# One sparse-attention and two-MoE kernel: a new hand-written order for the attention half, and the first loads put into one queue

## The chip, the cores and the metric

One Trainium2 chip, one core. The metric is the time of one execution of the whole program in microseconds (us); 0.2% of it is 2.2 us.

## The reference

```python
def _attn_ref(q, k, v, tau):              # q, k, v: (4, 8, 576, 64) float32
    scores = (1 / np.sqrt(64)) * np.matmul(q, k.transpose(0, 1, 3, 2))
    thresh = np.max(scores, axis=-1, keepdims=True) - tau
    scores = np.where(scores >= thresh, scores, -1000000000.0)
    scores = scores - np.max(scores, axis=-1, keepdims=True)
    attn = np.exp(scores)
    attn = attn / (np.sum(attn, axis=-1, keepdims=True) + 1e-09)
    return np.matmul(attn, v)

def _moe_ref(x, w_gate, w_val, w_out):    # x: (2304, 512), d_ff 1536
    return (1 / (1 + np.exp(-(x @ w_gate)))) * (x @ w_val) @ w_out

def _moe2_ref(x, w_in, w_out):            # d_ff 2048
    h = x @ w_in
    return (h * np.cos(h)) @ w_out

def reference(...):                       # attention -> (tokens, 512) -> moe -> moe2
    x = attn_out.transpose(0, 2, 1, 3).reshape(B * S, H * D)
    return _moe2_ref(_moe_ref(x, ...), ...)
```

The weights of the two MoE layers come in as float64.

## The kernel before

The 32 heads are worked in 16 **pairs** of heads. A pair has nine blocks of 128 queries: four for each head and one that holds the last 64 queries of both. Every product is made with split numbers: a float is a high part that TensorE takes in one pass and a low part, and two or three products are summed in PSUM.

The steps of one query block, with the letter that the tables of the kernel give them:

- S, four matmuls of 288 columns (six for the ninth block) into two PSUM banks, of which there are two pairs (L959, TensorE);
- M, the row's largest score (L965, VectorE, 128x576); E, the exponential (L970, ScalarE); Y, the threshold from M and tau (L813 on ScalarE, L817 on VectorE or L815 on GpSimd, by the table YS); K, mask, product and sum in one instruction (L973, VectorE);
- T and t, four transposes and one (L989, L996, TensorE); H and h, their high part copied out of PSUM (L899, ScalarE);
- the low part, by the table LOWS (LOWS_L for the small ones): V is a subtraction on VectorE (letters L and l, L910), G a copy on ScalarE (C, L914) and a subtraction on GpSimd (G, L919), T a matmul with minus the identity (N and n, L903, TensorE) and a copy on ScalarE (O and o, L906).

V is the product with the values (L1056, TensorE), folded by F on ScalarE and A on VectorE (L1026, L1031). R, U, X and x (L1136, L1147, L1163 to L1169) scale a pair's result and split it for the MoE product. Ahead of each pair its queries, keys and values are loaded, scaled (s), split into high (Q, J, Z) and low (q, j, z) parts and, but for the first pair, copied by DMA into the doubled layout that S reads (u, y, d). WHERE says for each pair which engine takes such a step (A ScalarE, D VectorE, P GpSimd). The letters 4, 5 (VectorE), w, 6 (ScalarE) and 7 (GpSimd) turn float64 weights into split floats. P are the matmuls of the first MoE layer (L564 to L566) that are laid between the pairs once two chunks of x are there, e their copies (L1214). D are four transposes into a spare bank that nothing reads (L825), put in after a block's S by the table FILL.

The class Plan collects these steps as tasks with what each needs. ORDER is a hand-written table: one string of letters for each engine, and the instructions of the attention half are issued on each engine in just that order. An engine works in order: an instruction that waits holds up all behind it. The second half (the rest of the MoE layers) has a table of its own, LATER.

The first pair has no DMA copies. `Pair.begin` issues its loads: tau (0.5 KB) and the first 128 queries (64 KB) on SyncE's queue, the first 640 key columns (320 KB) on ScalarE's queue; the other three pieces follow as tasks on SyncE's queue. VectorE makes `factor_q` and `off` from tau (L739, L740), ScalarE makes the high parts (`first_hi`: keys L657, queries L655, which read `factor_q`), VectorE the low parts (`first_lo`: L670, L674), GpSimd the plain key copy (`first_keys`, L683). Before that, TensorE makes 26 transposes of the identity into a bank that nothing reads:

```python
    for _ in range(26):
        nc.tensor.transpose(warm[:, 0:P], ident, ident)
```

Of the kernel before, what the change touches and what calls it, by code (L numbers as in the profile page):

```python
# [33 lines left out]
KW = 2 * S + SL  # L34
# [37 lines left out]
    DVE=(
        "jqMjqKqMMKKM4MK5MKYKMlMYYK4LL5MKYKllMMYlK4K5IlMMLKKM4l5KMMLKKlMML4K5KllMLMKLAYIlM4K5KMAMKLxlMA4KK5MYlMKxLM4K"
        "llK5MMYlLKKAM4lAI5KMLMYKK4M5MlKKLLMMAlKKALLLM4llM5IlKKLMA4l5MKAYKLMlMLKKLlMMKKALLAMllMKlAYKMLYAKIMLMlYKKLMMK"
        "lLKMMYlKKMALLllKAMMlLKKAMIlAMYKKlLMMLYKKMlAMKLYKAMLLlYlKMMlKYLKIlMMAKKAMLMlKKMMYKLAlMYLKKllLLMlAMLKKIMALMlAK"
        "KLMlMLKKLMlMYKKMMAllLLAKALKMLAMYlIKLKMMKYKMlYLKMLAYlMAKLLLMKllLKMMlLYKKIlAMMYLKKMjYlMAKKLMMlYKAKMLMKLLYAKllM"
        "YlMLLKIKlLAMMYYKKlMMALqKAlKMLLLAKMllMKLlMKAILKAlMMYYKKMlMYKYAKlAMLMKKMlYMlKKLMlMLKKIlAMMYKYKLMMAlKLMYlYKKMzA"
        "lKlMLLMAlYYILKKLlAMMYLYKKMMAlKYAKLMAlYKMLYLMllKKlMMKKLMMAlLIKKLMYlKAlMYMKYKALLAMMllAKKlILxlLAAUxAUxx"
    ),
    POOL=(  # L80
        "JJQYJYjYqZYzG7csQq7YJjYY7GYZ7YYzcGsQJ7qjUYsGXz7YQcUX7YqYJG7Y7jYYsYcQGZYqz7YJGY7GY7GjYUXZxYYsczQUXxGqJZYzYGjs"
        "cQGYJGYYqYGGYGjYsUcXYGQxZzJqGUXGxYjZYGQGqczYYZjsUXxYGzYcGGYYZUXxqzGYJjcGqYYGYJGcZzYqUGZzJjGYsGQGYZcUzXXxYxYJ"
        "GjGGGcYUYGsJjQGqYUYXxxGYGcsYQJqGzjGGGUcZGYGzUYGYGGGcYYGURRX"
    ),
    SP=(
        "10001W2uuuyWyuyy0ddssssW1uduuuW2ssssdyyrrW0y1RyssssRW2uu0uussssWrr1ddRRWyyy2yssssuuWgguu0Wssdssyydgg1WgyygDs"
        "sssrrWyggu2RRuugdrssrssuyd0RRyssssyggDu1u2d0gusygsrugss1dryyygsssysgRg2uuRu0dssssdg1ygurrgsgyyssRRsDuugg0ddu"
        "s2sssr1urygyyyDgg0ssssu2uRRyugyugDysssrrysgdg2ssssRRdu1gug0ssdrssdgguu2yDDgsyyrysssg10uuddRgssRssuugygyyy12s"
        "usssdguDrdryug0Ryussssr2rggD1RyssssdyRguu2uyRssss1yyudy0gsgDgssrrgRRs1gdys0gsdyrgrssguuuuDssyyDssgg2dgRRssss"
        "gg2uugrrdyyyuyusssRgsgRDssDssssssgrrRRgggDD"  # L90
# [1904 lines left out]
```

## Time and profile before

| | us |
|---|---|
| median of 3 runs | 1091.14 |
| lowest, highest | 1090.83, 1092.13 |
| the profiled execution, its own time | 1091.87 |
| its span | 1090.0 |
| TensorE busy | 1069.9 (98%) |
| VectorE busy | 911.8 (84%) |
| ScalarE busy | 763.3 (70%) |
| GpSimd busy | 545.0 (50%) |

The span is cut by what is done: attention and the first product up to about 385 us, the rest behind. PE, DVE, ACT, POOL and SP are TensorE, VectorE, ScalarE, GpSimd and SyncE; PEld are TensorE's weight loads. A busy share is an average, so each stretch is read by itself; in a row of the timeline the brackets tell how long the engine had been idle before an instruction, and what ended that. The 1.87 us between the span and the execution's time lie outside the profile.

### The profile page before, as it was taken

The page shows a single profiled execution, that of the slowest core. Times are in us where ns is not written, and L with a number is a line of the kernel's source. Part 1 is how long each engine was busy: PE and PEld are TensorE (multiplying, and loading weights), DVE is VectorE, ACT ScalarE, POOL GpSimd, SP SyncE. Part 2 cuts the span into 40 slices and gives each one's busy share as a digit, 9 for nine tenths or more (in the row PEclk, how much of TensorE's full clock was granted, in tenths as well). Part 3 has the DMA queues.
Part 4 walks back from the last instruction along what each step waited for, and adds up shares of the span by engine and source line. Part 5 has one row for each costly group of instructions (what it writes and reads, how often), then busy time and mean ns, then how long its engine had stood idle before and what let it go on. Part 6 is the DMA issues. An engine that isn't in the chain of part 4 may idle for free.

```text
span 1090.0 us, 17697 instructions
## 1 busy us (share of the span) xinstructions
PE 1069.9 (98%) x5774; PEld 911.6 (84%) x5774; DVE 911.8 (84%) x1650; ACT 763.3 (70%) x1488; POOL 545.0 (50%) x518
## 2 busy tenths in 40 slices
PE   7899999999999999999999999999999999999998
PEld 6788888888888888988888888888888888888886
DVE  7999998999888747878887657788779899889997
ACT  6999888888888744656654334368867677788773
POOL 6877877736775425342424252242344535445562
PEclk9999999999999999999999999999999999999999
DMA  6888788787777378998977554866444454557752
GB/s 194 233 227 243 223 225 229 203 234 219 209 203 201 94 231 305 302 335 305 312 232 232 178 180 149 282 210 215 157 155 155 159 185 159 195 192 276 265 203 87
DMA packets 94413, 234.05 MB, mean 215 GB/s; under 512 B 13178, under 2 KB 21490, under 8 KB 84594
## 3 DMA queue, kind: packets, MB, share of 16 engines
q1 hardware_dynamic: 94178, 232.60, 67.0%
q8 instruction: 46, 0.75, 0.3%
q14 instruction: 45, 0.37, 0.1%
q10 hardware_dynamic: 144, 0.33, 0.1%
HBM read 141.33 MB, written 59.84 MB: 185 GB/s over the span
## 4 chain that ended last, share of the span: by engine, by line
PE 85%; DVE 6%; ACT 3%; POOL 2%; DMA 2%; issue 2%; SPq 0%; ACTq 0%; DVEq 0%; POOLq 0%
PE h L1441 7%; PE h L1442 7%; PE h L1443 7%; PE s L959 6%; PE o L564 5%; PE o L565 5%; PE o L566 5%; PE v L1056 5%; PE h L1630 4%; PE t L989 4%; PE h L1631 4%; PE h L1632 4%; PE o L1750 4%; PE o L1751 4%; PE o L1752 4%; PE m L564 2%
## 5 line engine op out<-in xcount | busy, mean ns | idle before, releaser
L1676 POOL TENSOR_TENSOR g<-raws,g 128x512 fp32r<-128x512 f32 x68 | 94.6, 1400 | 139.8 <-ACT g L1675 117.7
L965 DVE TENSOR_REDUCE sm<-s 128x1 f32<-128x576 f32 x144 | 106.6, 751 | 9.5 <-PE s L959 7.5
L973 DVE SCALAR_TENSOR_TENSOR p<-s,sm,p 128x576 f32<-128x576 f32 x128 | 102.8, 813 | 8.8 <-ACT p L970 3.9
L1441 PE MATMUL h<-x,w 128*128 128x256 f32 (+1 forms) x304 | 101.4, 333 | 0.4 <-DVE raws L1718 0.4
L1442 PE MATMUL h<-x,w 128*128 128x256 f32 (+1 forms) x304 | 101.3, 333 | 0.0
L1443 PE MATMUL h<-x,w 128*128 128x256 f32 (+1 forms) x304 | 101.3, 333 | 0.0
L970 ACT ACTIVATE p<-s,sm 128x576 f32<-128x576 f32 x128 | 93.7, 741 | 9.8 <-DVE sm L965 9.2
L899 ACT ACTIVATE PT<-t 128x512 fp32r<-128x512 f32 (+1 forms) x160 | 86.1, 556 | 15.0 <-PE t L989 10.4
L959 PE MATMUL s<-kk,qh 128*128 128x288 f32 x320 | 92.3, 319 | 3.1 <-DVE p L973 2.0
L1056 PE MATMUL v<-PT,vn 128*128 128x256 f32 (+3 forms) x532 | 84.8, 302 | 0.2 <-ACT st L1214 0.2
L919 POOL TENSOR_TENSOR PT<-praw,PT 128x512 fp32r<-128x512 f32 x51 | 67.1, 1317 | 34.3 <-ACT praw L914 16.3
L1760 DVE TENSOR_TENSOR y<-o,y 128x512 f32<-128x512 f32 x120 | 78.7, 682 | 6.1 <-PE o L1752 5.9
L959 PE MATMUL s<-khi,ql 128*128 128x288 f32 x288 | 81.2, 296 | 1.0 <-DVE ql L670 0.6
L989 PE MATMUL t<-ident,p 128*128 128x128 f32 x512 | 76.9, 276 | 3.1 <-DVE PT L910 1.6
L1750 PE MATMUL o<-g,w 128*128 128x512 f32 x196 | 76.7, 392 | 0.5 <-ACT o L1766 0.5
L1751 PE MATMUL o<-g,w 128*128 128x512 f32 x196 | 76.4, 390 | 0.0
L1752 PE MATMUL o<-g,w 128*128 128x512 f32 x196 | 76.3, 389 | 0.0
L1630 PE MATMUL h<-form,w 128*128 128x512 f32 x192 | 75.0, 390 | 0.5 <-ACT side L1599 0.5
L1056 PEld LDWEIGHTS v<-PT,vn 128*128 128x128 f32 (+1 forms) x532 | 73.3, 186 | 2.2 <-DVE x L1031 0.5
L1631 PE MATMUL h<-form,w 128*128 128x512 f32 x192 | 74.7, 389 | 0.0
L1632 PE MATMUL h<-form,w 128*128 128x512 f32 x192 | 74.7, 389 | 0.0
L1675 ACT ACTIVATE g<-raws 128x512 fp32r<-128x512 f32 x106 | 64.3, 624 | 13.1 <-DVE raws L1718 8.3
(214 smaller groups left out, 3385.5 us busy)
## 6 DMA issues: line engine op xcount, KB each, us to landing
w<-wd SPq DMA_DIRECT2D x62, 1024.0 KB
wd<-stage SPq DMA_DIRECT2D x64, 512.0 KB
gd<-st SPq DMA_DIRECT2D x64, 256.0 KB
wraw<-in_moe_w_out_dram SPq DMA_DIRECT2D x28, 512.0 KB
qh<-qsplit SPq DMA_DIRECT2D x60, 144.0 KB
wraw<-in_moe_w_in_dram SPq DMA_DIRECT2D x16, 512.0 KB
spare<-gd SPq DMA_DIRECT2D x7, 1024.0 KB
early<-gd SPq DMA_DIRECT2D x7, 1024.0 KB
```

What stands on the lines that cost most here:

```text
L959: nc.tensor.matmul(s[:, half, 0:HALF], qq, keys[:, half * HALF:half * HALF + HALF], start=(i == 0), stop=(i == len(mms) - 1),)
L989: nc.tensor.matmul(tp[:, c * P:(c + 1) * P], self.pn[:, k0:k0 + P], ident, is_transpose=True, start=(c == 0), stop=(c == 3))
L1056: nc.tensor.matmul(o, w, x, start=z == 0, stop=z == len(steps) - 1)
L1441: nc.tensor.matmul(o, w_hi, x(0, c), start=begin, stop=False, **late)
L1442: nc.tensor.matmul(o, w_hi, x(1, c), start=False, stop=False, **late)
L1443: nc.tensor.matmul(o, w_lo, x(0, c), start=False, stop=c == KC - 1, **late)
L1630: nc.tensor.matmul(ps(), of(0, c), hi, start=fresh and c == 0, stop=False, skip_group_check=True)
L1631: nc.tensor.matmul(ps(), of(0, c), lo, start=False, stop=False, skip_group_check=True)
L1632: nc.tensor.matmul(ps(), of(1, c), hi, start=False, stop=c == 1, skip_group_check=True)
L1750: nc.tensor.matmul(ps(), of(0, c), hi, start=begin, stop=False, skip_group_check=True)
L1751: nc.tensor.matmul(ps(), of(0, c), lo, start=False, stop=False, skip_group_check=True)
L1752: nc.tensor.matmul(ps(), of(1, c), hi, start=False, stop=True, skip_group_check=True)
```

## The change

`ORDER` is another table: the five strings have other orders, and the tables that choose engines were drawn anew, so that the strings have other letters too. In the attention half, steps on each engine that differ in number, before to after:

| engine | steps |
|---|---|
| TensorE | D 9 to 13, N 18 to 17, n 3 to 4 |
| VectorE | L 91 to 98, l 93 to 92, U 2 to 5, x 6 to 8, j 3 to 4, q 4 to 3, z 1 to 0 |
| ScalarE | C 51 to 45, O 18 to 17, o 3 to 4, Y 29 to 40, X 4 to 8, Z 3 to 5, J 3 to 5, Q 6 to 4 |
| GpSimd | G 51 to 45, Y 62 to 51, U 15 to 12, X 12 to 8, x 10 to 8, Z 13 to 11, J 16 to 14, j 14 to 13, Q 12 to 14, q 14 to 15, z 15 to 16 |

The letters S, M, E, K, T, t, H, V, P and those of the weights are as many as before. The warm-up has 22 transposes for 26. The first keys go first on SyncE's queue, then the first queries, then tau. The diff, cut (a line of "..." stands for what is left out):

```diff
 ORDER = dict(
     PE=(
-        "SDDDDSTSNDDDSTSNtTSnTStNSTTNSTtDDNSTStVNTtSSTBVtTSNSTTSVTtSSTVtNNSTStVnTTtNSTVBStSTVSTVTNSNtSTTNNSPtTPPStPST"
...
+        "SDDDDSDSTDNSTtSNDDTStTnSNSTTDDSNTDDtNSTStDTNVtSTSnVBTtSnNSTTStVTTSSVtNNSTStTTVtTBSVNtSTnSNVSTSTVNtTTSNNNSPTP"
...
     ACT=(
-        "JQJQEYQsHEEOwHEOhECHo6EHhOEwHHHEOHhEOh6pHhEwEOHhCa6HEREhHwOEH6CHEEaahHwEYYHEHhOO6hHFhpEYoHHEhOwECFHRZhEYaHE6"
...
+        "QJJQQYEsJEHEOwHEOhECH6hEHZoOEwHHHEOQHEOhh6HhEwEOCHph6HoEEaRHhwOEoHC6HEEhsHaawHEEHhOOphHChEHH6hawEHRYFEOhXH6o"
...
 LOWS = (
-    "TTGTTVTTG VTGVVTVVT GVTTVTGVT VGVVVVGGV GVVVGVTGV VVVGGVGVG GVVGVVGVG GVGVVVVGV "
...
+    "TTGTTVTTG VTGVVTGVV TTGTTTGVT VVGVVVVVG GVVVGVTGV GVGVVVGVG VVVGVVGVG VGVGVVGVV "
...
 SHARED = (
-    "SSS. .S.S .... .... .... .... .... .... .... .... .... .... .... .... .... .... "
+    "SSSS .S.. .... .... .... .... .... .... .... .... .... .... .... .... .... .... "
...
 FILL = (
-    "421001001 000000000 000000000 000000000 000000000 000000000 000000000 000000000 "
+    "411110041 000000000 000000000 000000000 000000000 000000000 000000000 000000000 "
...
-    for _ in range(26):
+    for _ in range(22):
         nc.tensor.transpose(warm[:, 0:P], ident, ident)
...
-        def load(self, nm, part=None, queue=nc.sync):
+        def load(self, nm, part=None):
...
-            queue.dma_start(self.first_raw(nm, part), self.src[nm][NP + half][:, part.start - half * width:part.stop - half * width])
+            nc.sync.dma_start(self.first_raw(nm, part), self.src[nm][NP + half][:, part.start - half * width:part.stop - half * width])
...
         def begin(self):
 
+            qs, ks = [slice(0, P), slice(P, S), slice(S, 2 * S)], [slice(0, S + SL), slice(S + SL, KW)]
+            self.load("k", ks[0])
+            self.load("q", qs[0])
             nc.sync.dma_start(taus[:, 0:1], tau.to_broadcast([P, 1]))
-            qs, ks = [slice(0, P), slice(P, S), slice(S, 2 * S)], [slice(0, S + SL), slice(S + SL, KW)]
-            self.load("q", qs[0])
-            self.load("k", ks[0], nc.scalar)
```

The new kernel has one line more ahead of `begin`, so its line numbers are those of before plus one there.

Three places where the order is another. First, SyncE's queue at the start (x_97 and bc are the buffers of the first pair's loads, raw_q and raw_k those of the second pair). Before:

```order
L734 DMA taus<-in_tau_dram 128x1
L640 DMA x_97<-in_q_dram 128x128
L640 DMA bc<-in_k_dram 128x576
L640 DMA x_97<-in_q_dram 128x576
L640 DMA x_97<-in_q_dram 128x448
L636 DMA raw_q<-in_q_dram 128x576
L636 DMA raw_k<-in_k_dram 128x640
```

Now:

```order
L641 DMA x_97<-in_k_dram 128x640
L641 DMA x_97<-in_q_dram 128x128
L738 DMA taus<-in_tau_dram 128x1
L641 DMA bc<-in_k_dram 128x576
L641 DMA x_97<-in_q_dram 128x576
L641 DMA x_97<-in_q_dram 128x448
L637 DMA raw_q<-in_q_dram 128x576
L637 DMA raw_k<-in_k_dram 128x640
```

The key load of 640 columns has come over from ScalarE's queue to the front of this one, and tau stands third. Second, ScalarE's first steps (kk is the doubled key tile, qh_99 the first pair's queries). Before:

```order
L640 DMA x_97<-in_k_dram 128x640
L738 ACT_TABLE_LOAD
L738 ACTIVATE one<-halfpi 128x1
L657 ACTIVATE kk<-x_97 128x640
L655 ACTIVATE qh_99<-x_97,taus 128x128
L657 ACTIVATE kk<-bc 128x576
L655 ACTIVATE qh_99<-x_97,taus 128x576
L970 ACTIVATE p<-s,sm 128x576
```

Now:

```order
L739 ACT_TABLE_LOAD
L739 ACTIVATE one<-halfpi 128x1
L656 ACTIVATE qh_99<-x_97,taus 128x128
L658 ACTIVATE kk<-x_97 128x640
L658 ACTIVATE kk<-bc 128x576
L656 ACTIVATE qh_99<-x_97,taus 128x576
L656 ACTIVATE qh_99<-x_97,taus 128x448
L814 ACTIVATE sm<-sm,taus 128x1
L971 ACTIVATE p<-s,sm 128x576
```

The query step, which reads what VectorE makes of tau, now stands ahead of the key step. Third, VectorE's first steps (ql_101 are the low parts of the queries, s the scores, sm the row's largest). Before:

```order
L739 TENSOR_SCALAR taus<-taus 128x1
L740 TENSOR_SCALAR taus<-taus 128x1
L674 TENSOR_TENSOR kk<-x_97,kk 64x640
L670 SCALAR_TENSOR_TENSOR ql_101<-x_97,taus,qh_99 64x128
L965 TENSOR_REDUCE sm<-s 128x1
L674 TENSOR_TENSOR kk<-bc,kk 64x576
L670 SCALAR_TENSOR_TENSOR ql_101<-x_97,taus,qh_99 64x576
L973 SCALAR_TENSOR_TENSOR p,sums<-s,sm,p 128x576
L670 SCALAR_TENSOR_TENSOR ql_101<-x_97,taus,qh_99 64x448
```

Now:

```order
L740 TENSOR_SCALAR taus<-taus 128x1
L741 TENSOR_SCALAR taus<-taus 128x1
L675 TENSOR_TENSOR kk<-x_97,kk 64x640
L671 SCALAR_TENSOR_TENSOR ql_101<-x_97,taus,qh_99 64x128
L675 TENSOR_TENSOR kk<-bc,kk 64x576
L966 TENSOR_REDUCE sm<-s 128x1
L671 SCALAR_TENSOR_TENSOR ql_101<-x_97,taus,qh_99 64x576
L671 SCALAR_TENSOR_TENSOR ql_101<-x_97,taus,qh_99 64x448
L974 SCALAR_TENSOR_TENSOR p,sums<-s,sm,p 128x576
```

The second key piece now stands ahead of the first M (TENSOR_REDUCE), and the last query piece ahead of the first K.

On the way to the first P the strings of both kernels hold 27 S, 24 T, 12 t and 8 V on TensorE; before there are also 14 N, 2 n and 9 D, now 15 N, 4 n and 13 D. Up to the 27th M, VectorE has 2 L, 2 l and one x fewer, and 7 Y, one j and one U more. Up to the 27th E, ScalarE has one J, Q, s, X, C and O and two o more, and 5 Y and 2 h fewer. From the first P to the last, the letters of TensorE keep step: at each S the number of P and of V put out before it differs between the two kernels by 3 at most.

## Rows read from the trace of the kernel before

**Rows 1.** Busy time of each engine by stretch; in brackets instructions; PEclk is the granted clock.
```profile
core 0: us, PE busy (x) PEld busy (x) DVE busy (x) ACT busy (x) POOL busy (x), PEclk, DMA share, GB/s
0.00:20.00 20.00, 15.87 (x96) 13.64 (x96) 13.27 (x26) 12.47 (x22) 11.25 (x23) 1.00 0.57 175
20.00:71.00 51.00, 44.73 (x305) 37.96 (x304) 48.93 (x110) 47.00 (x105) 40.00 (x47) 1.00 0.87 230
71.00:400.00 329.00, 325.53 (x2080) 284.14 (x2079) 286.09 (x665) 272.64 (x595) 208.50 (x241) 1.00 0.74 209
400.00:1000.00 600.00, 599.36 (x2934) 507.66 (x2933) 483.55 (x729) 372.64 (x664) 239.22 (x178) 1.00 0.64 220
1000.00:1090.00 90.00, 84.44 (x368) 68.21 (x366) 79.92 (x123) 58.52 (x106) 46.04 (x32) 0.99 0.56 198
```

**Rows 2.** The same view from the first score to the first P.
```profile
8.00:71.00 63.00, 54.93 (x372) 46.34 (x373) 59.36 (x128) 55.57 (x120) 46.33 (x54) 1.00 0.80 215
```

**Rows 3.** Timeline of the first ten us: start, us, engine, line, what, idle before.
```profile
0.73 0.38 SPq L734 DMA_DIRECT2D taus<-in_tau_dram  x1
...
1.35 5.30 PE L599 MATMUL warm<-ident 128*128 128x128 f32 x26 [1.35 <-POOL halfpi L477]
...
5.06 0.15 DVE L739 TENSOR_SCALAR taus<-taus 128x1 f32<-128x1 f32 x1 [1.97 <-DMA taus<-in_tau_dram]
...
5.45 0.74 ACT L657 ACTIVATE kk<-x 128x640 fp32r<-128x640 f32 x1 [2.79 <-DMA x<-in_k_dram]
5.50 1.66 POOL L683 TENSOR_SCALAR khi<-x 64x576 fp32r<-64x576 f32 x3 [2.17 <-DMA x<-in_k_dram]
...
6.09 0.39 ACT L655 ACTIVATE qh<-x,taus 128x128 fp32r<-128x128 f32 x1
6.21 0.84 DVE L674 TENSOR_TENSOR kk<-x,kk 64x640 fp32r<-64x640 f32 x1 [0.94 <-ACT kk L657]
6.40 0.68 ACT L657 ACTIVATE kk<-bc 128x576 fp32r<-128x576 f32 x1
7.08 0.34 DVE L670 SCALAR_TENSOR_TENSOR ql<-x,taus,qh 64x128 fp32r<-64x128 f32 x1
...
8.03 0.40 PE L959 MATMUL s<-khi,ql 128*128 128x288 f32 x1 [0.46 <-POOL khi L683]
...
8.73 0.76 DVE L965 TENSOR_REDUCE sm<-s 128x1 f32<-128x576 f32 x1 [1.30 <-PE s L959]
9.52 0.76 DVE L674 TENSOR_TENSOR kk<-bc,kk 64x576 fp32r<-64x576 f32 x1
...
10.20 0.82 DVE L670 SCALAR_TENSOR_TENSOR ql<-x,taus,qh 64x576 fp32r<-64x576 f32 x1
```

**Rows 4.** Waits of VectorE from 8 to 71 us: in total, times, longest.
```profile
DVE sm L965 <- PE s L959: 2.1, 3, 1.3
```

**Rows 5.** Waits of TensorE from 71 to 400 us.
```profile
PE t L989 <- DVE PT L910: 1.4, 2, 0.9
```

**Rows 6.** Groups of instructions by shape, 0 to 110 us: busy us, mean ns, idle before.
```profile
L910 DVE TENSOR_TENSOR PT<-t,PT 128x512 fp32r<-128x512 f32 x14 | 9.6, 687 | 0.8 <-ACT PT L899 0.7
L817 DVE TENSOR_SCALAR sm<-sm,taus 128x1 f32<-128x1 f32 x10 | 2.0, 211 | 0.1
L1169 DVE TENSOR_TENSOR xs_a<-x,xs_a 128x512 fp32r<-128x512 f32 x2 | 1.8, 922 | 0.0
L813 ACT ACTIVATE sm<-sm,taus 128x1 f32<-128x1 f32 x8 | 2.2, 288 | 0.0
L703 ACT ACTIVATE vn<-raw_v 128x640 fp32r<-128x640 f32 x1 | 0.7, 721 | 0.0
L914 ACT ACTIVATE praw<-t 128x512 f32<-128x512 f32 x9 | 5.4, 601 | 0.1
L825 PE MATMUL warm<-ident 128*128 128x128 f32 x36 | 4.4, 272 | 0.0
```

**Rows 7.** Line L1169 (step x) over the whole span, by engine: ns least, median, most.
```profile
L1169 DVE TENSOR_TENSOR xs_a<-x,xs_a x6: 674/685/1157, 62.6 to 385.8; 128x512 fp32r<-128x512 f32 x6
```

More of the change, by code (lines that the diff above doesn't have):

```diff
@@ new lines @@
+        "EEFOwaCEHHFOhEHHH6OOOwEECehhH6pehHEEFHwhFOERH6eYEEehHeZwEHECH6heFHEEHHFwehhHp6eEhFEHHCewhECH6FEReHhHEEYhHese"
+        "EYFEHHCHFhhHEFOhEFHpHCEehCHEYERHheeECHHehEYEFsHHEYeEHhhFHCephHEEHhFZFCREHYYEHeheYEEHHCFYhHEEYeFhhHHeYEEChHeF"
+        "HHCpEhHYeEZREeChHEHFeHECYEFheHEEHHhhFpHCEehEHeFHhZRFEEYHheHEEHHCheEECHeFEhhHHFYhEFHYXFHCHEEYhHpeCERECehHEHHe"
+        "EhYFHHHFhhEeYHCEHeehhEYEpHFRheHEEHFeHEEChFHEHYEHJeEYHFhEhHCEhHeECHhFYpHREYEFhCHeHHCEEhFFHHHEXhhHXEYeChHFpEYY"
+        "hEeCFHEHEReHEhYEeHCFHEhFYECHHHeJEHhheEehpHCHEEeFhHXYFRHeEYEHehEhEYCHeeEECFHHHFphhHhEeEHHehFHYREECheHEFHHEFCh"
@@ L71 @@
+        "EFCHHHhhEYeHEehHHYpEEhFCHeEYCEFRHhEHChYEHeEFFHHEEHFhhHhpHeHXXFheFFbX"
     ),
     DVE=(
[L73 to L76, printed above, removed]
@@ L79 @@
+        "lLMMYAKKlLMMLKKLMlYMKKMMAllLLAKlALKMLYMAKKlIMMYYKKlMMKLLMlAKLLALMllYKKLMMllYKIKLAMMYLKKLAlMMLKKlMMYKLKAMMYKL"
+        "LlAKlMMYKlLMlKIALMKUAlKMLMYKlKAMLLLKMALllKMjlAIMKlKMMYAKLKMMLYlKKMALMlYKKALLMYMKlLlKlMMYLKIlALKAxLMMYKKLMMlY"
+        "KKMMlYYKALKLAllMLlMIKKLLMlAMLKKlMYMKYALKMAlYKMALLllMKLKlMLLMKlKAIMMKYKMlAKMlMYLKKAMAYMLYLLlAlLKKlILxxLAlAAUU"
+        "xx"
     ),
     POOL=(
-        "JJQYJYjYqZYzG7csQq7YJjYY7GYZ7YYzcGsQJ7qjUYsGXz7YQcUX7YqYJG7Y7jYYsYcQGZYqz7YJGY7GY7GjYUXZxYYsczQUXxGqJZYzYGjs"
@@ L82 @@
[L82 to L90 removed]
+        "JJQjqYY7zcsYYqG7YZGJ7jYGzc7YYQJqZG7Ux7zGcYX7YsQqJ7YjYGs7YYczGQ7Y7YqJG7UjYXGZzcQYxqYUXYGGJGjYGYZczYQqYYJGGsjz"
@@ new lines @@
+        "YUcQXGJqXGxYGjsYYQGYzGcJYYjqYzGUsXQYYxGYcqGUJxjGGZYzcsQJGqGjZzYYYGUsQcZqGjYGsGQYzqcYJxGxGGYGUZcsGQXYzjqUxZzs"
+        "GcGJQjqGYYZzYGGcYGUZzYGGYcGUURRX"
+    ),
+    SP=(
+        "10001W2uyyyyWuu0udsdssWsuu2d1Wuussss0yWyyrr1yd2ssssWuuRRdd0ssssWrryy1yRRWuuy2ssssWuudg0gWsssudgsyrugr1yWyyss"
+        "sgsugRWuRuu2ggdDsssgrr0sydgyRRssssyy1dDgDD0gugssssuuu12ggyyyyssdss2ugrr0uguusgsssdyRRry1yrggdyssRRssg2u0uugg"
+        "ydDdsssus1yDgryrggyus2sssugRR0uyudssggrrys1dsRyRssssguyd2ggyydussssy10guuyggssr2rsusdgygygyRssssRrr1ugug0ydu"
+        "ss2ssDdguu0dyRRusDsssu1yggs2sssydyruurgssssuDyydRR1rygg0yruDssssggRRyugg0uu2ssgusyys1g2yddsgrgssrsgyDRyssssy"
+        "2RudrdguuuggssssryRRgDssDgssssssrrggRRDDDgg"
@@ L635, in load @@
                 self.raw[nm] = at.tile([P, src.shape[1]], F32, tag=f"raw_{nm}", name=f"raw_{nm}")
-                queue.dma_start(self.raw[nm], src)
+                nc.sync.dma_start(self.raw[nm], src)
                 return
```

33 lines of the change are left out of this document (14 added, 19 removed).

## The prediction

> **What bounds the kernel now.** I read the stretches first, then the first ten us, then the waits. The reader should see three things in the stretches [rows 1]. From 71 us on TensorE is the bound: it is busy 325.53 of 329 us up to 400 us and 599.36 of 600 up to 1000. Nothing that another engine does better there can give more than the 3.5 us that TensorE is idle from 71 to 400. Between 20 and 71 us it is busy 44.73 of 51 us only, while VectorE is busy 48.93 and ScalarE 47.00: there the softmax steps set the pace. In the first 20 us TensorE's 15.87 us are partly for show, since they hold the 26 warm-up transposes, 1.35 to 6.65 us [rows 3], and fillers that nothing reads (36 records in the whole stretch, [rows 6]). The granted clock is 1.00 in all stretches but the last (0.99), so it is at its upper level, 2.4 GHz, and the clock plays no part.
>
> So the change can act in three places only: the start (before the first score), the softmax-bound stretch up to the first P at 71 us, and the few idle us of TensorE behind it. The second half follows its own unchanged table, and TensorE is full there: what the attention half gains or loses arrives at the end one for one.
>
> **What does not change.** TensorE's useful work is the same: as many S, T, t, V and P, and N and n are 21 together in both. On the way to the first P there is one N and two n more, behind it as many fewer, so this cancels. The four warm-up transposes that go end before 6.65 us, when TensorE had nothing to do till after 7 us, so they are worth nothing; if the first score came earlier they would be a small gain. The four new fillers are 16 transposes. Before, 16 of them took about 1.9 us, and TensorE idles 63.00 - 54.93 = 8.1 us from 8 to 71 us [rows 2]. They fit into that; where a score is ready behind one, it waits for at most one group of four, some 0.5 us. I cost both at 0, between 0 and +0.5.
>
> **The start.** I follow VectorE, since it is the engine that the first scores queue on [rows 3]. Before: tau, first in its queue (issued 0.73), lets VectorE begin at 5.06; the first keys let ScalarE begin at 5.45; VectorE then does key low part (6.21), query low part (7.08), waits for the score, M at 8.73, second key low part at 9.52, and is through with these at 10.20. Now ScalarE does the query step first, and that needs tau. Let tau land at T. The two tau steps of VectorE begin at T and take 0.15 us with the second just behind, so say 0.23; then ScalarE's query step holds it for 6.40 - 6.09 = 0.31; its key step begins at T + 0.54. VectorE followed that step by 6.21 - 5.45 = 0.76: T + 1.30. Then key low part (7.08 - 6.21 = 0.87), query low part (0.34), the rest of the score (8.73 - 8.03 = 0.70, with 0.04 to begin), M (9.52 - 8.73 = 0.79): T + 4.04. The second key low part (10.20 - 9.52 = 0.68) lies inside the 0.74 us in which the score is made, where VectorE had idled 1.30 us. Before, the same work was done at 10.20. The gain is 10.20 - T - 4.04 = 6.16 - T. GpSimd's key copies would not hold it up: the score waited for them to 8.03, and T + 2.55 is later than that.
>
> What is T? Not before 5.06, where it landed as first of its queue: gain 1.1 us at most. Not after 6.40, when ScalarE already used the second key piece, which stood third in the queue as tau does now: a loss of 0.24 at worst. In front of tau now stand 320 KB, which landed by 5.45 beside other loads, and 64 KB. That is the nearest row, so I take T = 5.6: **-0.56 us**, from -1.1 to +0.24. The order that follows (two query pieces before the first K, 0.82 us) neither adds nor removes work.
>
> **Up to the first P.** Up to the 27th M, VectorE loses two L (0.687 each) and one x (0.922) and gains seven Y (0.211 each) and one j and one U; these two have no row here, and I price them at the x, which also reads two tiles of SBUF: -1.37 - 0.92 + 1.48 + 1.84 = +1.0 us, a little less for two small l that go [rows 6]. ScalarE gains J, Q and s (0.721 each, by the copy of 640 columns), C, X and O (0.601 each) and loses five Y (0.288 each); two o and two h are of one size and cancel: 2.16 + 1.80 - 1.44 = +2.5 us [rows 6]. GpSimd is relieved, but it was busy only 46.33 of 63 us and nobody named it as the bound.
>
> Now the slack: VectorE idles 63.00 - 59.36 = 3.64 us from 8 to 71, of which 0.73 lie before the first M and belong to the start, so 2.9 [rows 2]. Its waits that have a name are small: 2.1 us for scores, 1.3 of them the first [rows 4]. ScalarE idles 7.4 us. A better order can take away the idle time of VectorE and no more; if all went, the stretch would be 2.9 - 1.0 = 1.9 us shorter. If ScalarE's 2.5 us came on top, it would be 2.5 longer. Nothing in the rows says which part of the idle goes; I take half, 1.45 - 1.0: **-0.4 us**, from -1.9 to +2.5.
>
> Step x shows a cost of such a move. On VectorE it took 0.685 us in the median and 1.157 at most [rows 7], with equal shapes, so something else held it for 0.47 us. The Trainium skill, page "SBUF — State Buffer", section "SBUF: two separate sides", gives a reason: GpSimd and VectorE share a port pair, and whichever of a GpSimd instruction and a VectorE instruction with two SBUF inputs starts first keeps it to its end. The trace agrees so far as 1.157 stands against 0.685. By that rule this change, which has four more such steps on VectorE (three U, two x and one j more, one q and one z fewer), would pay 4 x 0.47 = 1.9 us of VectorE's time, an estimate, a quarter of it before the first P, and the sum would come to about 1090.9.
>
> **From the first P to the end of attention.** TensorE idles 3.47 us there [rows 1]; the largest named part is 1.4 us for VectorE's low parts [rows 5]. VectorE gets more to do: over the whole attention seven L (4.8 us) and four steps of the x kind (2.7 to 3.7), of which about 1 us was counted above, so some 6.5 to 7 us on top of 286.09 in 329. It stays below nine tenths. GpSimd's six G fewer make room for others. Bounds: -3.5, if TensorE never waits, and +1.4, if its waits for VectorE double. I take **+0.2 us**, since the load grows by two hundredths only.
>
> **Sum.** -0.56 - 0.4 + 0.2 = -0.76 us. The profiled execution took 1091.87 us (span 1090.0 and 1.87 outside), so it would take 1091.11. It was 0.73 above the median 1091.14, so against the median the forecast is **1090.4 us**: no change that can be told, since about 0.2%, 2.2 us, is what a measurement can tell here.
>
> **Rivals.** *The order takes the waits away.* Then VectorE has no idle time up to 71 us (-1.9), TensorE's named waits for it behind that go (-1.4), and the start gains as above (-0.56): -3.9, 1087.3 us. For it: those waits are there, and what comes before the first P is worth its full size. Against it: VectorE is already busy 59.36 of 63 us and gets more work. Chance 0.33.
>
> *The added load comes onto the path.* ScalarE is busy 47.00 of 51 us from 20 to 71 us; with 2.5 more it has 1.5 left, which is less than what an engine that works in order loses in waits. It would then be the bound: +2.5, and VectorE's added steps double TensorE's waits behind 71 us (+1.4), less the start (-0.56): +3.3, 1094.5 us. It decides from the point where ScalarE's idle time before the first P would have to fall below 1.5 us. Against it: ScalarE's waits there may be just what the new order shortens. Chance 0.15.
>
> *The new order does nothing.* TensorE is busy 98% of the span and its order is almost the same (at each S the numbers of P and V before it differ by 3 at most); the start's gain could be lost again at the first place where VectorE was not late. Then 1091.1 us. Chance 0.15.
>
> **Numbers.** My forecast has 0.37, and with the rival of no effect 0.52 for a time within 0.2%; faster by more 0.33, slower by more 0.15. The range reaches a little beyond the faster rival, 1087.0, and up to 1093.4, short of the slower rival's full price; about one in ten is left out at either end.
>
> **What would show it.** Right, if in the new profile tau's steps on VectorE begin near 5.6 us, the first M ends near 9.6 us with the second key low part already done, the first P comes within 2 us of 71 us, and TensorE is busy about 325 of 329 us behind it. The start is wrong if tau lands after 6.2 us. The middle is wrong if VectorE's idle time up to the first P is well above or below 1.5 us, or if ScalarE's waits shrink while TensorE's grow. If the first P comes 3 us earlier the faster rival holds; if ScalarE is busy almost without a gap and the first P comes later, the slower one.

## The result: slower by 0.6%

| | executions | median us | lowest to highest | ratio to the kernel before, 95% |
|---|---|---|---|---|
| before, beside it | 4 | 1091.64 | 1090.83 to 1093.0 | |
| changed | 4 | 1098.55 | 1096.04 to 1098.76 | 1.0058 [1.0046, 1.0070] |
| changed, again | 6 | 1097.87 | 1096.23 to 1100.08 | 1.0063 [1.0050, 1.0075] |

The forecast was 1090.4 us. The profiled execution of the changed kernel took 1096.04 (span 1094.2 against 1090.0), so it shows 4.2 us of the loss; the other 2 to 3 us lie in longer executions, two of which later traces caught. All line numbers of the changed kernel are those of before plus one.

The stretches of the changed kernel, as in [rows 1] and [rows 2]:

```profile
core 0: us, PE busy (x) PEld busy (x) DVE busy (x) ACT busy (x) POOL busy (x), PEclk, DMA share, GB/s
0.00:20.00 20.00, 15.98 (x99) 14.00 (x100) 14.33 (x32) 13.82 (x25) 9.00 (x19) 1.00 0.70 196
20.00:71.00 51.00, 45.02 (x311) 38.47 (x309) 45.95 (x107) 46.96 (x104) 35.11 (x40) 1.00 0.89 219
71.00:400.00 329.00, 322.77 (x2064) 280.76 (x2063) 291.01 (x670) 272.50 (x600) 191.40 (x222) 1.00 0.73 205
400.00:1000.00 600.00, 599.40 (x2932) 507.31 (x2931) 483.19 (x727) 372.23 (x664) 237.19 (x177) 1.00 0.64 222
...
8.00:71.00 63.00, 55.67 (x386) 47.73 (x385) 57.40 (x130) 57.07 (x122) 39.23 (x45) 1.00 0.86 216
```

From 71 to 400 us TensorE is idle 6.23 us where it was 3.47, and this is the stretch in which idle time costs its full size. Its longest waits there, where [rows 5] had one kind of 1.4 us:

```profile
PE s L960 <- DVE p L974: 1.7, 3, 1.3
PE t L990 <- DVE LT L911: 1.1, 2, 0.9
PE t L997 <- DMA xd<-x: 1.0, 1, 1.0
PE t L1104 <- DVE PT L911: 0.6, 1, 0.6
```

To say where the time goes I use one measure all through, the **lag**: TensorE's instructions but for warm-ups and fillers, 5712 records in every trace, each at the median duration of its line and shape, are summed; the lag is how much later than the kernel before a trace reaches the same share of the sum. "Repaired" is the last kernel below. The moment is the one in the kernel before.

| trace (its time, us) | 20 | 32 | 50 | 74 | 92 | 116 | 250 | 270 | 370 | 390 | 1000 |
|---|---|---|---|---|---|---|---|---|---|---|---|
| new start only (1090.0) | -0.2 | -0.2 | -0.8 | -1.3 | -1.1 | -1.1 | -1.7 | -1.7 | -1.6 | -1.7 | -1.9 |
| changed (1096.0) | -0.8 | +0.9 | -0.9 | +0.6 | +2.9 | +3.1 | +2.1 | +3.3 | +2.8 | +4.1 | +4.4 |
| changed (1099.3) | -1.2 | -0.2 | -2.5 | +0.0 | +2.3 | +3.8 | +2.7 | +7.5 | +6.9 | +8.2 | +7.7 |
| repaired (1093.4) | -1.1 | +0.1 | -2.2 | +0.2 | +0.1 | +0.9 | -0.2 | +0.9 | +0.5 | +1.3 | +1.8 |

Four losses stand out in the trace of 1096.0. **From 26 to 34 us** the start's lead goes. ScalarE now makes the third pair's query copy (L704), waits 0.92 us for its data, and the exponential behind it is late for VectorE:

```profile
26.98 0.68 ACT L704 ACTIVATE qsplit<-raw_q 128x576 fp32r<-128x576 f32 x1 [0.92 <-DMA LZ<-LT]
...
28.04 0.73 ACT L971 ACTIVATE p<-s,sm 128x576 f32<-128x576 f32 x1
...
28.88 0.82 DVE L974 SCALAR_TENSOR_TENSOR p<-s,sm,p 128x576 f32<-128x576 f32 x1 [1.19 <-ACT p L971]
```

What the place costs goes with this wait: in the four traces of the changed kernel it is 0.92, 0, 0.23 and 0.63 us, and the lag grows from 20 to 34 us by 1.3, 0.1, 0.3 and 0.8. At 32 us every trace of the new order, also the two without the copy on ScalarE, stands about 1 us later than at 30, and 0.5 to 0.7 of that is back at 34.

**From 74 to 87 us** two weight steps of VectorE (letter 5, L521) take 1.93 and 2.00 us, where the median of 68 is 0.684. Each began within 0.15 us after a subtraction of GpSimd and ended 0.55 us after it; TensorE then waited for what stood behind them:

```profile
75.41 1.44 POOL L711 TENSOR_TENSOR ql<-raw_q,qsplit 128x576 fp32r<-128x576 f32 x1
...
75.47 1.93 DVE L521 SCALAR_TENSOR_TENSOR wt<-we,wt 128x512 uint32<-128x512 uint32 x1
...
77.92 0.63 PE L990 MATMUL t<-ident,p 128*128 128x128 f32 x4 [0.90 <-DVE LT L911]
...
83.80 1.59 POOL L711 TENSOR_TENSOR klo<-raw_k,khi 128x640 fp32r<-128x640 f32 x1
...
83.94 2.00 DVE L521 SCALAR_TENSOR_TENSOR wt<-we,wt 128x512 uint32<-128x512 uint32 x1
...
86.94 0.37 PE L960 MATMUL s<-kk,qh 128*128 128x288 f32 x1 [1.28 <-DVE p L974]
```

**Near 259 us** TensorE waits 0.98 us for GpSimd's zeros (L984), which end at 259.51; the profile names a transfer (below). **At the end of attention**, 370 to 390 us, VectorE waits for a high part of x that GpSimd makes (X); the kernel before has such an X on GpSimd here too, at 377.20 us. But two steps x (L1170) now stand together in VectorE's queue, and behind them a low part (L) that TensorE needs:

```profile
380.99 1.29 DVE L1170 TENSOR_TENSOR xs_a<-x,xs_a 128x512 fp32r<-128x512 f32 x2 [0.91 <-POOL xs_a L1166]
382.20 0.68 DVE L911 TENSOR_TENSOR PT<-t,PT 128x512 fp32r<-128x512 f32 x1
...
383.04 0.41 PE L1104 MATMUL t<-ident,bc 128*128 128x128 f32 x2 [0.65 <-DVE PT L911]
```

### The profile page after: what moved, and what is told of

Read it like the earlier page. It is cut to its first block, busy times and chain, and to the rows that moved or that the text cites. A ratio compares the mean times of both kernels' runs of the same rounds, so it can differ in the third digit from the quotient of the medians.

```text
span 1094.2 us, 17711 instructions
## 1 busy us (share of the span) xinstructions
PE 1072.1 (98%) x5786; PEld 912.4 (83%) x5786; DVE 918.6 (84%) x1660; ACT 767.9 (70%) x1499; POOL 521.3 (48%) x491
## 4 chain that ended last, share of the span: by engine, by line
PE 51%; DVE 2%; DMA 1%; ACT 1%; issue 0%; ACTq 0%
PE h L1442 5%; PE h L1444 5%; PE h L1443 5%; PE h L1631 4%; PE h L1632 4%; PE h L1633 4%; PE o L1751 4%; PE o L1752 4%; PE o L1753 4%; PE o L566 3%; PE o L567 3%; PE o L565 3%; DMA early<-gd 1%; PE o L1842 1%; PE o L1841 1%; PE o L1843 1%
## 5 line engine op out<-in xcount | busy, mean ns | idle before, releaser
L920 POOL TENSOR_TENSOR PT<-praw,PT 128x512 fp32r<-128x512 f32 x45 | 58.5, 1301 | 39.7 <-ACT PT L900 22.1
L990 PEld LDWEIGHTS t<-ident,p 128*128 128x128 f32 x512 | 58.8, 140 | 18.9 <-DVE PT L911 3.2
```

The lines of the kernel that those rows point to most:

```text
L990: nc.tensor.matmul(tp[:, c * P:(c + 1) * P], self.pn[:, k0:k0 + P], ident, is_transpose=True, start=(c == 0), stop=(c == 3))
```

## Experiments

Seventeen runs follow: thirteen new kernels, the changed kernel three times more, and one of the thirteen again. Strings are shown with the letters around the edit. Ratios are to the kernel before in the same sitting.

### The start and the table apart

The kernel before with the new loads (keys, queries, tau on SyncE's queue) and 22 warm-ups, then with 26; the changed kernel with the old loads and 26; with the new loads and 26; with 32.

```diff
-    for _ in range(22):
+    for _ in range(26):
```

> The kernel before with the new start alone: keys, then queries, then tau, all in the sync queue, 22 warm-up transposes; its order and places as before. Theory (the start is worth what its trace shows, and more of it is kept where the order is the old one): first exponent 0.5 to 1.0 us earlier, end 0 to 0.8 us earlier, 1090.8 to 1091.6. Rival (the old order gives the lead back at the first wait for a transfer): within 0.2 us. Rival (the new load order itself makes later loads late): 1 us or more slower, and then part of the 7 us is the start's.

Measured: 1090.97 us (1089.26 to 1091.87), ratio 0.9992 [0.9984, 1.0001].

> The kernel before with the new start and 26 warm-up transposes. Theory (the start gives 0.6 us, warm-up counts for nothing): 1090.4 to 1091.1 beside 1091.1 to 1091.6 of the kernel before. If the low clock at 8 to 12 us cost the run with 22 something: 0.3 to 0.8 us less than that run.

Measured: 1091.76 us (1089.47 to 1092.81), 0.9998 [0.9990, 1.0007].

> The changed kernel with the loads of the kernel before at the start (tau, then queries in the sync queue, keys in ScalarE's queue) and 26 warm-up transposes, so the new order and places alone. If the start is worth its 0.6 us to the end: 1098.5 to 1099.2. If the order takes the start's lead back at 27 us whatever it is: 1097.6 to 1098.4. If the new load order is part of the loss: under 1097.

Measured: 1096.38 us (1095.92 to 1099.35), 1.0051 [1.0039, 1.0063].

> The changed kernel with 26 warm-up transposes in place of 22. In two of five traces with 22 the granted clock of TensorE was 0.5 to 0.7 from 8 to 12 us; in the trace before, with 26, it was 1.00. Theory (the executions that take 2.6 us more than the profiled one are those with the low clock at the start): median 1096 to 1096.7 and a mean granted clock of 0.999 to 1.0 in every execution. Rival (the lower clock falls where TensorE waits anyway, and the 2.6 us come from elsewhere): median within 0.7 us of 1098.

Measured: 1094.91 us (1094.68 to 1097.87), 1.0037 [1.0025, 1.0049]; mean clocks from 0.998 to 1.0.

> The changed kernel with 32 warm-up transposes in place of 22 (with 26 its median was 1094.9 us beside 1097.9 and 1098.6). Theory of the clock (over the executions of the new order the time goes with the mean granted clock: at 1.0 eight executions average 1094.6 us, at 0.998 and under 1097.5): every execution at a mean clock of 0.999 or 1.0, median 1094 to 1095.5. Rival (the number of warm-ups only shifts the phase of what follows, and 26 happened to fall well): anything between 1095.5 and 1098.5, whatever the clock.

Measured: 1097.11 us (1094.46 to 1098.54), 1.0047 [1.0034, 1.0060]; mean clocks from 0.998 to 1.0.

What follows: with the old table the new start is worth from 1.7 us gained to 0.1 lost (22 warm-ups), or from 1.1 gained to 0.8 lost (26), and so none of the loss; the new table with the old loads costs 5 us. That the new loads are part of the loss, as my rule for the old loads under 1097 us would have it, does not hold, since with 26 warm-ups the new loads are no slower than the old. The theory of the warm-ups fell: 26 came out faster than it said, 32 slower. Yet in the new table the number seems to count: 26 measured 1.0037 [1.0025, 1.0049] where the changed kernel with 22, run again, measured 1.0063 [1.0050, 1.0075], while in the old table 26 were no faster than 22. So some 2.5 us of the loss may hang on the warm-ups and the new table together; how is not shown, and five executions are few, since those of one and the same kernel of this family lie up to 7 us apart. Kernels with 26 warm-ups are therefore set beside 1.0037 below, and those with 22 beside 1.0063.

### The two weight steps

```diff
-...MMY4KK5llMMlYYLKKAI4lMA5KMLMKK...   (VectorE)
+...MMY45KKllMMlYYLKKAI4lM5AKMLMKK...
```

> The changed kernel with two weight steps (the one that joins an exponent and a mantissa word) moved ahead of where they ran beside a subtraction of GpSimd: the first in front of the two masks that stood before it, the second in front of one halved sum. Theory of the port: both steps take 0.69 us in place of 1.93 and 2.00, TensorE's waits of 0.90 us at 77.9 and 1.28 us at 86.9 go, and the time falls by 1.5 to 2.5 us, to 1096 to 1097. Rival (VectorE has room and the 2 us come back as other waits before 400 us): within 0.5 us of the changed kernel.

Measured: 1096.82 us (1093.70 to 1101.09), 1.0052 [1.0034, 1.0070]. Timeline of its VectorE and GpSimd:

```profile
72.49 0.69 DVE L521 SCALAR_TENSOR_TENSOR wt<-we,wt 128x512 uint32<-128x512 uint32 x1
81.14 0.68 DVE L521 SCALAR_TENSOR_TENSOR wt<-we,wt 128x512 uint32<-128x512 uint32 x1
...
74.64 1.44 POOL L711 TENSOR_TENSOR ql<-raw_q,qsplit 128x576 fp32r<-128x576 f32 x1
81.94 1.60 POOL L711 TENSOR_TENSOR klo<-raw_k,khi 128x640 fp32r<-128x640 f32 x1
```

The same steps, the same GpSimd instructions, only not side by side: 0.69 and 0.68 us, and both waits of TensorE gone. From 74 to 92 us its lag goes from -0.7 to -0.7, where the changed kernel's goes from +0.6 to +2.9: the two places cost 2.3 us, shown. All nine traces of the new table that leave the two steps there have them at 1.75 to 2.03 us; none of the seven that move them has one held there. The traced executions differ by as much at the end, 2.5 us (1093.70 against 1096.23). The medians differ by 1.05 us only, short of what the theory said; with six executions from 1093.70 to 1101.09 the two intervals overlap, so that what arrives end to end is not told by this run. Part of it goes again near 110 us, as the next pair of runs shows.

### Where the gain goes again: the weight loads

The two steps, the third pair's query copy back on GpSimd, and in the last pair the low part ahead of the two steps x:

```diff
-    Q="APAPPPPPPPPPPPPP"
+    Q="APPPPPPPPPPPPPPP"
-...HEOQHEO...   (ScalarE)
+...HEOHEO...
-...zcsYYqG...   (GpSimd)
+...zcsQYYqG...
-...KKlILxxLAlAAUUxx   (VectorE)
+...KKlILLxxAlAAUUxx
```

> The two weight steps moved as in the run before, and besides the third pair's query copy back from ScalarE to GpSimd (where it stood in the kernel before) and, in the last pair, one low part drawn ahead of two key parts that wait for GpSimd. Theory: also VectorE's wait of 1.19 us at 28.9 goes (0.5 to 1.1 us kept from the start's lead) and TensorE's 0.65 us at 383; altogether 3 to 4 us less than the changed kernel, 1094.5 to 1095.5. Rival (only the port counts): as the run with the two steps alone. Rival (the new order as a whole, not single waits): within 0.5 us of the changed kernel.

Measured: 1096.15 us (1092.60 to 1098.94), 1.0042 [1.0025, 1.0058]. Its lag at 92 us was +0.1, the changed kernel's +2.9; at 116 us it was +3.1 against +3.1. Timeline of its ScalarE:

```profile
98.08 0.69 ACT L514 ACTIVATE we<-wraw 128x512 f32<-128x512 f32 x1 [1.27 <-DMA wraw<-in_moe_w_val_dram]
...
107.25 0.66 ACT L514 ACTIVATE we<-wraw 128x512 f32<-128x512 f32 x1 [1.91 <-DMA wraw<-in_moe_w_val_dram]
```

The buffer for a piece of weights (512 KB) exists once, so a piece is loaded only when the one before has been read: here the twelfth was issued at 99.85 us and read from 107.25 on. A faster attention comes to the last two pieces before their loads do, and ScalarE, which works in order, stands. So I moved their conversions behind:

```diff
-...HHFwehhHp6eEhFEHHCewhECH6FEReH...   (ScalarE)
+...HHFehhwHp6eEhFEHHCehECHwFE6ReH...
-...LLAL4K5llMMLlKKALMIl4Y5MKAYKLl...   (VectorE)
+...LLALK4ll5MMLlKKALMIlYMK45AYKLl...
```

> The three repairs, and the conversions of the eleventh and the twelfth weight piece placed three and seven steps later on ScalarE and one and two steps later on VectorE, where their loads have landed (with the three repairs ScalarE waited 1.27 us at 98 and 1.91 us at 107 for these two loads, and the lead of 2.9 us over the changed kernel at 92 us was gone at 117 us). Theory (a second bound, the chain of weight loads, took the lead back): both waits go, the lead at 117 us stays at 2 to 3 us, and the time falls 1.5 to 3 us below the run with three repairs, 1093 to 1094.7. Rival (the new order loses time everywhere between 100 and 400 us): within 0.5 us of that run, 1095.7 to 1096.7.

Measured: 1095.84 us (1091.96 to 1098.72), 1.0037 [1.0026, 1.0049]: the rival's number beside the run with three repairs. Beside the changed kernel, with 22 warm-ups in both, it is faster all the same (1.0063 [1.0050, 1.0075]). The twelfth load, issued at 100.4 us, landed later still, and another wait took the place. ScalarE and TensorE of this run:

```profile
109.06 0.68 ACT L514 ACTIVATE we<-wraw 128x512 f32<-128x512 f32 x1 [0.53 <-DMA wraw<-in_moe_w_val_dram]
...
111.63 0.33 PE L997 MATMUL t<-ident,p 128*128 128x128 f32 x1 [1.15 <-ACT rs L1128]
```

That the loads take gain back near 110 us is shown by these waits; how much differs: from 92 to 116 us the lag grows by 2.9 us with the three repairs, by 1.6 with the two steps alone and by 0.6 in the repaired kernel, whose ScalarE waits 3.2, 2.3 and 1.3 us for the two loads. How to keep it is not shown: my one try failed. In that run the lag also grew by 1.3 us from 20 to 34 us: with the query copy on GpSimd a threshold behind it was late, and VectorE waited 0.84 us for that. So the copy can cost time on either engine.

### More of the same kind, and the late waits

The second trace of the changed kernel ("again") had two more such places. Its VectorE and GpSimd:

```profile
49.14 1.43 POOL L711 TENSOR_TENSOR ql<-raw_q,qsplit 128x576 fp32r<-128x576 f32 x1
...
55.90 1.44 POOL L1148 TENSOR_TENSOR x<-x,bc 128x576 f32<-128x576 f32 x1
...
49.20 1.91 DVE L521 SCALAR_TENSOR_TENSOR wt<-we,wt 128x512 uint32<-128x512 uint32 x1
...
56.12 1.51 DVE L518 TENSOR_SCALAR wt<-wraw 128x512 uint32<-128x512 uint32 x1
```

In the run with 26 warm-ups it was the low keys, one of the steps that the change gives to VectorE:

```profile
55.35 1.45 POOL L1148 TENSOR_TENSOR x<-x,bc 128x576 f32<-128x576 f32 x1 [0.42 <-ACT we L514]
...
55.41 2.07 DVE L711 TENSOR_TENSOR klo<-raw_k,khi 128x640 fp32r<-128x640 f32 x1
```

In the trace of 1096.0 neither happened: GpSimd's steps there follow a transfer and begin 1.6 and 0.9 us behind VectorE's, where in the second trace they began 0.06 and 0.22 us ahead. Summed over VectorE's steps that took 0.2 us more than their shape's median, the time lost by 71 us is 0 and 2.8 us in the first two traces of the changed kernel, and from 71 to 400 us 2.6 in both. The kernel before has it too: 1.6 us up to 71 us, in two weight steps and the x of [rows 7]. So three groups of edits on the kernel with 26 warm-ups: the port repairs (the two steps and those at 48 and 55 us), the late repairs (in GpSimd's queue near 258 us the zeros c ahead of a query copy Q, and the low part of the last pair as above), and both.

```diff
-...4KK5llMYlKLLIlM4jMKYKA5...   (VectorE, port)
+...45KKllMYlKjLLIlMMK4YKA5...
-...GUsQcZqGj...   (GpSimd, late)
+...GUscQZqGj...
```

> The changed kernel with 26 warm-ups, and VectorE's steps moved off GpSimd's long ones before 90 us: the weight steps at 48, 75 and 84 us ahead of the two masks or the half before them, the low keys at 55 us ahead of two low parts, the shift at 55 us behind two maxima and a mask. Theory of the port: none of VectorE's weight steps over 0.8 us, TensorE's waits at 59, 78 and 87 us gone, 2.5 to 3.5 us of lead over the run with 26 warm-ups at 92 us; of that the loads at 100 to 110 us take a part back, and the time is 1 to 2.5 us less, 1092.5 to 1094. Rival (all is taken back by the loads): 1094.4 to 1095.7.

Measured: 1095.86 us (1094.92 to 1097.62), 1.0046 [1.0034, 1.0058].

> The changed kernel with 26 warm-ups and two repairs after 250 us: in GpSimd's queue the zeros beside the local scores ahead of a query copy that waits for a transfer (TensorE waited 0.9 to 1.4 us behind it at 259 us in six of seven traces of this order, 0.24 in one), and in the last pair one low part ahead of two key parts. Theory (these waits lie on the path, nothing is behind to hide them): 1.2 to 1.9 us less than the run with 26 warm-ups, 1093 to 1094.2. Rival (the next wait takes their place): within 0.5 us of it, 1094.4 to 1095.7.

Measured: 1096.69 us (1093.91 to 1098.52), 1.0054 [1.0041, 1.0068].

> Both groups of repairs with 26 warm-ups. If their gains add: 2.2 to 4 us less than the run with 26 warm-ups, 1091 to 1092.8, that is the kernel before within 0.2%. If the second hides the first: as the better of the two alone. If it comes out under 1090.5, the new order is better than the old one once these places are mended.

Measured: 1094.37 us (1091.71 to 1095.82), 1.0024 [1.0015, 1.0033].

Each alone is no faster than the 26 warm-ups; that speaks for "the next wait takes its place", or for the spread of five executions. Together they are clearly faster than the changed kernel, 1.0024 [1.0015, 1.0033] beside 1.0063 [1.0050, 1.0075]; beside the kernel that has the 26 warm-ups alone, 1.0037 [1.0025, 1.0049], the intervals overlap, so what both groups add to the warm-ups is not settled. All of my numbers for the three were too low, by 1.6 to 2.5 us.

### The longer executions

> The changed kernel once more, unaltered, for a second trace: three of its four executions so far took 1098.5 to 1098.8 us, the profiled one 1096.0. If the extra 2.6 us belong to the order (a queue or a shared port that goes one way or the other from run to run), a trace of 1098.6 us shows one stretch that is 2 us longer or more than in the trace at hand, with waits of 1 to 2 us in it; the theory of the port expects it where VectorE's weight steps and GpSimd's subtractions start within 0.2 us of each other. If the extra is spread (transfers or the clock), no stretch of 50 us differs by more than 0.5 us. Time 1098.5 either way, 1.0058 of the kernel before.

Measured: 1097.87 us, but the traced execution took 1096.23, as the first had; its lag is within 0.4 us of the first trace's from 270 us on. It settled nothing on the longer ones.

> The changed kernel unaltered, for one more trace. Theory (an execution draws its waits: up to 2.8 us of VectorE behind GpSimd before 71 us, 0 to 1.9 us for the weight load near 108 us, 0.2 to 1.4 us near 259 us): a trace of 1098 us or more has two or three of these, and no stretch beyond them is over 0.5 us longer than in the trace of 1096.0. Rival (the loss lies after attention, in transfers of the second half): the traces agree up to 400 us within 1 us and part behind it.

Measured: 1099.31 us.

> As the run before, the same kernel once more: by the theory, if it is slow it differs from the fast traces at those places; if all four traces of this kernel come out near 1096 us and the executions without a trace near 1098.5, then tracing itself picks the fast ones and the 2 to 3 us cannot be seen in a trace.

Measured: 1098.93 us.

> The kernel with both groups of repairs and 26 warm-ups once more, for a second trace (its first, of 1091.7 us, had none of VectorE's steps behind GpSimd; nine executions without a trace took 1092.8 to 1095.8). Theory: a trace of 1094 us shows a wait of 1 us or more near 108 us (the weight load) or a step of VectorE behind GpSimd near 32 or 72 us. Rival: as above, nothing to be seen.

Measured: 1092.73 us, with no such wait.

Two long executions, traced. At 250 us their lags are within 1.4 us of those of the two shorter traces; from 250 to 270 us one loses 4.8 us and the other 3.6 against the kernel before, the two shorter ones 1.2 and 0.5. GpSimd and TensorE of the longest:

```profile
258.70 0.75 POOL L691 TENSOR_SCALAR raw_q<-raw_q,taus 128x576 f32<-128x576 f32 x1 [3.18 <-DMA raw_q<-in_q_dram]
260.94 0.67 POOL L706 TENSOR_SCALAR qsplit<-raw_q 128x576 fp32r<-128x576 f32 x1 [1.50 <-DMA LZ<-LT]
261.58 0.45 POOL L984 TENSOR_SCALAR pl<-pl 128x64 f32<-128x64 f32 x2
...
258.76 0.39 PE L567 MATMUL m<-xs_a,w 128*128 128x512 f32 x1
262.08 0.33 PE L997 MATMUL t<-ident,pl 128*128 128x128 f32 x1 [2.93 <-POOL pl L984]
...
263.44 0.63 PE L565 MATMUL m<-xs_a,w 128*128 128x512 f32 x1
```

The zeros that TensorE waits for (L984) stand in GpSimd's queue behind the scaling and the copy of the next queries, and these wait for transfers. What it costs is more than the wait: the granted clock falls behind it, and the product that took 0.39 us takes 0.63. Stretches of the same trace:

```profile
255.00:260.00 5.00, 4.15 (x25) 3.39 (x23) 4.60 (x11) 3.59 (x8) 1.26 (x2) 1.00 0.98 216
260.00:265.00 5.00, 2.92 (x10) 2.38 (x11) 2.17 (x6) 1.06 (x3) 3.21 (x5) 0.75 0.33 97
265.00:270.00 5.00, 4.98 (x33) 4.46 (x32) 2.94 (x7) 3.71 (x7) 3.02 (x3) 0.91 0.86 241
```

So the zeros alone were put ahead of both, in the changed kernel as it is, and in the one with the port repairs, the last pair's repair and 26 warm-ups ("repaired"):

```diff
-...GUsQcZqGj...   (GpSimd)
+...GUcsQZqGj...
```

> The changed kernel as it is (22 warm-ups, no other repair) with one step moved: in GpSimd's queue near 258 us the zeros beside the local scores ahead of the scaling and the copy of the next queries. Theory (this place makes the slow executions slow): no wait of TensorE near 260 us, no granted clock under 1.0 after 20 us, executions within 2 us of one another, and a median of 1094.8 to 1096 us, that is 2 to 3 us under the changed kernel's 1098. Rival (the transfers that are late there make the next step wait): within 0.7 us of 1098.

Measured: 1097.57 us (1095.89 to 1099.06), 1.0059 [1.0046, 1.0072].

> The port repairs, the low part in the last pair and 26 warm-ups as in the run with both groups (median 1094.4, trace 1091.7), with the zeros ahead of the scaling too and not only of the copy. Theory: median 1091.5 to 1093, executions within 2 us. Rival (its spread has another cause): 1094 to 1094.8.

Measured: 1093.67 us (1092.99 to 1097.58; eleven of twelve from 1092.99 to 1094.26), 1.0022 [1.0014, 1.0030].

In the trace of the first, the wait is gone and the clock stays:

```profile
255.54 0.46 POOL L984 TENSOR_SCALAR pl<-pl 128x64 f32<-128x64 f32 x2
256.20 0.75 POOL L691 TENSOR_SCALAR raw_q<-raw_q,taus 128x576 f32<-128x576 f32 x1 [0.20 <-DMA raw_q<-in_q_dram]
...
260.00:265.00 5.00, 4.96 (x33) 4.11 (x33) 4.54 (x11) 4.09 (x9) 4.12 (x4) 1.00 0.46 123
```

But this kernel's other four executions took 1097.5 to 1099.1: the place explains the two long traces, and it is not the only thing that makes an execution long. That theory fell as a whole. What the rest of these four lost in stays open, for no trace shows it.

With these repairs and 26 warm-ups the new order comes from 1.0063 to 1.0022, that is some 4.5 of 6.9 us; 2.8 of these the kernel with the 26 warm-ups alone had too, so the moved steps by themselves may be worth from nothing to some 3 us here (with 22 warm-ups in both, the three repairs and the moved pieces came to 2.8). Its trace of 1093.37 tells where the rest goes: 1.2 us of the start's lead by 32 us, 0.8 at the end of attention and 0.5 in the second half (the table of lags). Between 32 and 370 us gains and losses nearly cancel: it gains 2.3 us up to 50, loses 2.4 up to 74, gains 0.4 up to 250, loses 1.1 up to 270 and gains 0.4 up to 370. TensorE's idle time from 71 to 400 us is 4.39 us there, near the 3.47 of before:

```profile
71.00:400.00 329.00, 324.61 (x2074) 282.98 (x2075) 290.21 (x671) 273.17 (x601) 192.03 (x222) 1.00 0.73 207
```

No version beat both kernels beyond doubt; the old order with the new start, 0.9992 [0.9984, 1.0001], is the best.

## Why the prediction was wrong

**The bound: right.** What TensorE lost before 400 us arrived at the end, +4.1 us at 390 and +4.4 at 1000.

**The start, -0.56: right** (-0.8 at 20 us). The tau steps began at 5.50 (I took 5.6), with the second key low part before the first M:

```profile
5.50 0.15 DVE L740 TENSOR_SCALAR taus<-taus 128x1 f32<-128x1 f32 x1 [2.42 <-DMA taus<-in_tau_dram]
...
6.85 1.26 POOL L684 TENSOR_SCALAR khi<-bc 64x576 fp32r<-64x576 f32 x1 [1.88 <-DMA bc<-in_k_dram]
...
7.61 0.64 DVE L671 SCALAR_TENSOR_TENSOR ql<-x,taus,qh 64x128 fp32r<-64x128 f32 x1
...
8.28 0.76 DVE L675 TENSOR_TENSOR kk<-bc,kk 64x576 fp32r<-64x576 f32 x1
...
9.06 0.76 DVE L966 TENSOR_REDUCE sm<-s 128x1 f32<-128x576 f32 x1
```

M ends at 9.82, not 9.6: the query low part took 0.64 us in place of 0.34; it began within GpSimd's key copy (to 8.11) and ended 0.14 us behind it. The warm-ups, which I put at nothing, may not be nothing: with 22 the granted clock was 0.57 to 0.59 from 8 to 12 us in three of nine traces, with 26 or 32 below 1.00 in one of ten (0.63), and the two with the new table and 22 that had it were at -0.4 at 20 us, the other six at -0.8 to -1.8. How much of the start reaches the end is open: with the old table the lag at 1000 us was -1.9 in the trace with 22 warm-ups and +0.8 in that with 26.

**Up to the first P, -0.4: wrong, +1.4** (from -0.8 at 20 to +0.6 at 74 us; the first P at 72.14, where it was 71.12):

```profile
71.12 0.40 PE L564 MATMUL m<-xs_a,w 128*128 128x512 f32 x1
...
72.14 0.40 PE L565 MATMUL m<-xs_a,w 128*128 128x512 f32 x1
```

"I take half" of VectorE's idle time was the step that failed: the rows did not say what would go, and I let a better order take it. VectorE's idle time grew from 3.6 to 5.6 us of 63, and its busy time, which I had grow by 1.0, fell by 2.0. ScalarE got busier by 1.5 us (2.5 forecast), but in this trace what cost time was not its load: it was one copy given to it that waits for its data. In the other three traces of the changed kernel the stretch costs 1.0 to 2.2 us, of which 0.1 to 0.8 go at this copy and 0.9 to 1.4 between 34 and 74 us; what takes the latter is not shown. VectorE was held beside GpSimd for 1.2 to 2.3 us there, but the repaired kernel, without that, loses 0.8 as well.

**First P to the end, +0.2: wrong, +3.5** (from +0.6 at 74 to +4.1 at 390 us), beyond my bound of +1.4. The step that failed is "since the load grows by two hundredths only": I priced an order by how busy an engine is. VectorE's busy time grew by 4.92 us, less than the 6.5 to 7 that I had, and 2.55 of these were the two weight steps that stood beside GpSimd: as many steps as before, in another place. I had the mechanism in hand at step x [rows 7] and applied it to the four added steps alone, at 0.47 us each, the excess of one chance case. The excess is up to 1.32 us, since a step that starts just behind a GpSimd instruction waits for its end. By the Trainium skill, page "SBUF — State Buffer", section "SBUF: two separate sides", whichever starts first keeps the shared pair for its whole instruction; the traces agree, with ends 0.55 us behind GpSimd's where such a step alone takes 0.684. My 1090.9 by that page was too low because I counted instructions and did not look where they stand.

**The faster rival**, which I gave the largest chance beside the forecast, needed VectorE without idle time up to 71 us and TensorE's named waits gone: VectorE idles 5.6 us there, and TensorE's idle time behind it grew from 3.47 to 6.23. **The slower rival** had the sign and 1094.5 us, but not the cause: it needed ScalarE's idle time under 1.5 us before the first P, and that was 63.00 - 57.07 = 5.9. **The rival of no effect** fails at the weight steps.

**The sum against the median.** I set the profiled execution beside the median with 0.73 us between them. For the changed kernel that distance is 2.5 us (1096.04 against 1098.55), the other way: twelve executions lie from 1096.0 to 1100.1. The two long ones that were traced lose it near 259 us, behind the zeros; for the others it is open.

## What to carry to other kernels

An order written by hand is not priced by counts of steps or by shares of busy time: lay VectorE's steps on SBUF beside what GpSimd does at that moment, and price a step that starts just behind a GpSimd instruction with the whole rest of that instruction: 1.2 to 1.3 us here. In a queue that works in order, put what another engine is about to need ahead of a step that waits for a transfer. Removing one such wait often only shows the next (a load, another queue), so read several executions, and trust the trace for where and the median for how much.
